# Attention and two mixtures of experts on one core: the first pairs' q sum, the start of their scores, and who does the shared work

## The chip, the cores and the metric

One core of one Trainium2 chip runs the whole program. The metric is device time in microseconds. Three runs of the kernel before took 885.33, 886.92 and 887.47 us; the median is 886.92.

## What is computed

Three layers run one after the other, in float32, on 4 sequences of 576 tokens, 8 heads of 64:

```python
# attention, for every sequence and head
q_d, k_d, v_d = (x.reshape(B, H, Sd, 4, D).mean(axis=3) for x in (q, k, v))
out_d = sm_attn(q_d, k_d, v_d)            # softmax(q_d k_d^T / 8) v_d
out_up = np.repeat(out_d, 4, axis=2)
mask = np.abs(pos[:, None] - pos[None, :]) < 4
out_local = softmax(where(mask, q k^T / 8, -1e9)) v
x = out_up + out_local                    # then to 2304 tokens x 512
# gated layer, 512 -> 1536 -> 512
x = (silu(x @ w_gate) * (x @ w_val)) @ w_out
# one of 8 experts for each token, 512 -> 1024 -> 512
out[mask] = gate_w[mask, None] * (np.maximum(x[mask] @ w1[e], 0) @ w2[e])
```

Down-sampling averages groups of four rows; the scores of the down-sampled attention are products of such averages.

## The kernel before, in words

**Order.** Every piece of work is a generator that yields the engine and the ns it expects to need. A list scheduler in the program (`Sched`, line 92) plays these against each other when the program is built, always taking what can start earliest and, among what is ready, the smallest priority; the instructions are issued in the order so found. At run time each engine goes through its own queue in that order. Line 281 marks work that either VectorE or GpSimd can do ("V"): the planner gives it to the one that would finish first (line 195). Such work is marked `how=True`: the planner does not let it run on VectorE while GpSimd works, nor the other way round (line 187). Copies out of PSUM are fixed to ScalarE.

**Attention.** A pair is two heads of one sequence on 128 partitions; there are 16, four for each sequence. `heads` (line 495) takes five tiles, loads q and k (lines 509, 510), then two layouts of v (lines 513, 514), and creates the tasks of the pair; the planner creates them after it has planned the load of v. The first four pairs (n < 4) use `local_e` and `down_e` in two parts each: part 0 holds the first 256 tokens. `local_e` makes banded scores in units of 58 queries (L724, L730), a softmax (L733 to L747), and turns the result with matmuls (L754). `down_e` sums k in groups of four (L651, L653), makes scores with four strided slices of q accumulated in PSUM (L672), a softmax (L675 to L690), transposes (L697), and a product with v (L707). `down_v` sums v (L547, L549). `piece_e` multiplies the banded weights with v (L782) and adds both (L789). The later pairs use `scores` (where q and k are summed by a reduction, L557), `local`, `down` and `values`.

**Gated layer.** Tokens go in 9 chunks of 256. `x_piece` splits a chunk's x into a high and a low part (L891, L893). The weights come in 6 blocks, each of two pieces of w_gate, w_val and w_out; `decode` (line 377) makes a high and a low part of each piece (L396, L400, L404, L407, L415, L417). `gemm1` (L936 for the very first block, L955) and `gemm2` (L987) use three products for each matmul. For chunks 0 and 1 the blocks alternate between the two chunks, so that one block of weights serves both as it comes in; chunk 2 and later follow. Chunk 2 is the first that needs the second sequence, pairs 4 to 7. `act_h` (L904 to L913) is the nonlinearity between `gemm1` and `gemm2`. Then come routing (line 1059) and the experts.

**Priorities.** `HEAD_P` (line 243) holds one for each pair, `WEIGHT_P` (line 250) one for each weight block: 1.0, 2.0, 3.0, 4.0, 4.5, 4.8. Smaller goes first. Pairs 4 to 7 stand at 1.4, 1.5, 1.6 and 1.7, between block 0 and block 1. Part 1 of a pair stands 0.5 behind part 0. Four pairs can hold tiles at a time.

**Fillers.** `keep_warm` (line 359) lets TensorE multiply zeros wherever the planner finds it free, until the first piece of x exists.

Of the kernel before, what the change touches and what calls it, by code (L numbers as in the profile page):

```python
# [19 lines left out]
ALU = mybir.AluOpType  # L20
# [45 lines left out]
def t_dve(n): return 62 + 1.045 * n  # L66
# [22 lines left out]
BOTH = ("DVE", "POOL")  # L89


class Sched:
# [61 lines left out]
    def advance(self, k, val):  # L154
        self.cur = k
        while True:
            try:
                r = k.gen.send(val)
            except StopIteration:
                break  # L160
            val = None
            if r[0] == "op":
                if k.eng == r[1] == "PE" and k.t == k.end + self.LAT["PE"]:
                    k.t = k.end
                k.ns, k.eng, k.rp, k.how = r[2], r[1], k.prio if r[3] is None else r[3], r[4]
                for eng in BOTH if r[1] == "V" else r[1:2]:
# [29 lines left out]
    def here(self, eng, k):  # L196

        if k.eng != "V":
            return True
        a, b = (self.first(e, k) + n for e, n in zip(BOTH, k.ns))  # L200
        return (a <= b) == (eng == BOTH[0])

    def run(self):
        while True:
            while self.runq:
                self.advance(*self.runq.pop(0))
            best = None
# [12 lines left out]
            start, eng, k = best  # L220
            ns = k.ns
            if k.eng == "V":
                for e, n in zip(BOTH, k.ns):
# [19 lines left out]
HEAD_P = [0.0, 0.1, 0.2, 0.3, 1.4, 1.5, 1.6, 1.7, 16.0, 17.0, 18.0, 19.0, 36.0, 37.0, 38.0, 39.0]  # L243
# [9 lines left out]
def build(tc, a):  # L253
# [241 lines left out]
    def heads(n):  # L495
# [14 lines left out]
        nc.sync.dma_start(out=sk[:, 0:SP6], in_=src[:, SP6:2 * SP6])  # L510
        sc.cur.t -= sc.LAT_DMA
# [3 lines left out]
        pr = sc.cur.prio  # L515
        if n < NV:
            sc.spawn(pr, local_e(n, 0, sq, sk, sv, sa))
            sc.spawn(pr, down_e(n, 0, sq, sk, sd, sa))
            sc.spawn(pr, down_v(n, sk, sd))
            sc.spawn(pr + REST_P, local_e(n, 1, sq, sk, sv, sa))  # L520
            sc.spawn(pr + REST_P, down_e(n, 1, sq, sk, sd, sa))
        else:
            sc.spawn(pr, down_v(n, sk, sd))
            sc.spawn(pr, scores(n, sq, sk, sa))
            sc.spawn(pr, values(n, sq, sk, sv, sa))
# [50 lines left out]
    def down(n, sq, sk, sp):  # L576
# [24 lines left out]
        for h2 in range(2):  # L601
# [7 lines left out]
            yield op("ACT", t_actp(2 * G))  # L609
            nc.scalar.copy(eT[:, h2], tp[:GH, 0:2 * G])  # L610
# [33 lines left out]
    def down_e(n, part, sq, sk, sd, sa):  # L644

        kd, up = (sq[:, SP6 + i * G:SP6 + (i + 1) * G] for i in (1, 2))
# [51 lines left out]
        yield op("ACT", t_actp(4 * w))  # L698
        nc.scalar.copy(eT, tp[:GH, 0:4 * w].rearrange("p (k g) -> p k g", k=2))
# [8 lines left out]
        yield op("ACT", t_actp(w))  # L708
        nc.scalar.copy(up[:, g0:g1], av[:, 0:w])
# [4 lines left out]
    def local_e(n, part, sq, sk, sv, sa):  # L714
# [40 lines left out]
        yield op("ACT", t_actp(k))  # L755
        nc.scalar.copy((sv[:, 640:640 + k], sa[:, 680:680 + k])[part], tp[:, 0:k])
# [7 lines left out]
    def piece_e(n, i, sq, sv, sa):  # L764
# [34 lines left out]
    def values(n, sq, sk, sv, sa):  # L799
# [4 lines left out]
        for jj, t in enumerate(T):  # L804
# [7 lines left out]
            yield op("ACT", t_actp(k))  # L812
            nc.scalar.copy(t, tp[:, 0:k])
# [23 lines left out]
        yield op("ACT", t_actp(G))  # L837
        nc.scalar.copy(up, av)
# [178 lines left out]
    def route_m(c, m, sv, lp):  # L1017
# [5 lines left out]
        yield op("ACT", t_actp(DM), hi)  # L1023
        nc.scalar.copy(row, xp)
# [11 lines left out]
        yield op("ACT", t_actp(DM), hi)  # L1036
        nc.scalar.copy(x2T[:, 0:DM], xp)
# [204 lines left out]
    def load_slot(e, j, tb, xhr, xlr):  # L1242
# [21 lines left out]
        yield op("ACT", t_actp(KD * m), -0.5)  # L1264
        nc.scalar.copy(xhr[:, :, js], pv)
# [166 lines left out]
    def rest_act(e, m, ps, hr):  # L1432
# [8 lines left out]
        for h in range(2):  # L1441
# [5 lines left out]
            yield op("ACT", t_actp(4 * m), -0.5)  # L1447
            nc.scalar.copy(h3[0][:, h], pt[:, 0:4 * m])
# [179 lines left out]
```

## Time and profile before

| | us |
|---|---|
| median of three runs | 886.92 |
| the profiled execution | 885.85 |
| its span, first to last instruction | 884.0 |
| TensorE busy (matmuls) | 865.4 |
| VectorE busy | 482.6 |
| ScalarE busy | 383.5 |
| GpSimd busy | 113.1 |

In the profile PE is TensorE's matmuls, PEld its weight loads, DVE VectorE, ACT ScalarE, POOL GpSimd, SP the queue that issues most loads. Line 672 has 96 matmuls in the code and 192 instructions in the profile: two for each of these float32 products. Matmuls are pipelined and their ends are modelled, so two neighbours can overlap by some ns; the start times are the firmer figures. L672 is line 672 of the kernel above. "<-" names what ended an idle time.

### The profile page before, as it was taken

The page shows a single profiled execution, that of the slowest core. Times are in us where ns is not written, and L with a number is a line of the kernel's source. Part 1 is how long each engine was busy: PE and PEld are TensorE (multiplying, and loading weights), DVE is VectorE, ACT ScalarE, POOL GpSimd, SP SyncE. Part 2 cuts the span into 40 slices and gives each one's busy share as a digit, 9 for nine tenths or more (in the row PEclk, how much of TensorE's full clock was granted, in tenths as well). Part 3 has the DMA queues.
Part 4 walks back from the last instruction along what each step waited for, and adds up shares of the span by engine and source line. Part 5 has one row for each costly group of instructions (what it writes and reads, how often), then busy time and mean ns, then how long its engine had stood idle before and what let it go on. Part 6 is the DMA issues. An engine that isn't in the chain of part 4 may idle for free. (4 is left out here: it accounts for less than half of the span.)

```text
span 884.0 us, 17461 instructions
## 1 busy us (share of the span) xinstructions
PE 865.4 (98%) x7122; PEld 775.7 (88%) x7123; DVE 482.6 (55%) x1163; ACT 383.5 (43%) x923; POOL 113.1 (13%) x115
## 2 busy tenths in 40 slices
PE   9999999999999999999999999999999999999995
PEld 5788889989999999889999999999888888888894
DVE  4999988665476466555333433474455544545210
ACT  2987778543353243333221322355345444444221
POOL 0102200011010010010010000101320330331211
PEclk9999999999999999999999999999999999999998
DMA  8663525312102111120000000354465554553100
GB/s 268 229 206 131 157 90 211 95 39 80 57 26 57 56 27 55 56 80 2 1 25 1 25 1 13 106 190 125 142 207 166 176 175 153 163 183 122 36 27 29
DMA packets 52629, 88.13 MB, mean 100 GB/s; under 512 B 7806, under 2 KB 24574, under 8 KB 52544
## 3 DMA queue, kind: packets, MB, share of 16 engines
q1 hardware_dynamic: 47664, 76.72, 27.1%
q0 software_dynamic: 4160, 9.48, 3.2%
q8 instruction: 57, 0.93, 0.4%
q10 hardware_dynamic: 720, 0.77, 0.3%
q14 instruction: 28, 0.23, 0.1%
HBM read 77.96 MB, written 10.57 MB: 100 GB/s over the span
## 5 line engine op out<-in xcount | busy, mean ns | idle before, releaser
L955 PE MATMUL ps<-xhi,w 128*128 128x256 f32 x1504 | 296.1, 288 | 1.4 <-DVE th L908 0.6
L955 PEld LDWEIGHTS ps<-xhi,w 128*128 128x128 f32 x1504 | 242.2, 191 | 5.2 <-issue 1.3
L955 PE MATMUL ps<-xlo,w 128*128 128x256 f32 x752 | 212.5, 283 | 0.0
L955 PEld LDWEIGHTS ps<-xlo,w 128*128 128x128 f32 x752 | 143.9, 191 | 1.5
L1304 PE MATMUL ps<-xh,w 128*128 128x336 f32 (+1 forms) x512 | 124.0, 315 | 0.0
L987 PE MATMUL x<-w,hh 128*128 128x512 f32 x384 | 120.8, 396 | 0.0
L906 DVE SCALAR_TENSOR_TENSOR th<-th,ps 128x256 f32<-128x256 f32 x108 | 45.0, 418 | 123.9 <-ACT th L904 123.6
L904 ACT ACTIVATE th<-ps 128x256 f32<-128x256 f32 x108 | 41.2, 382 | 150.5 <-PE ps L955 150.0
L1304 PEld LDWEIGHTS ps<-xh,w 128*128 128x128 f32 x512 | 88.2, 188 | 2.2
L1192 DVE TENSOR_TENSOR w<-w,w 128x1024 fp32r<-128x1024 f32 x64 | 76.8, 1217 | 22.7 <-ACT w L1189 22.5
L1304 PE MATMUL ps<-xl,w 128*128 128x336 f32 (+1 forms) x256 | 79.8, 312 | 0.0
L987 PEld LDWEIGHTS x<-w,hh 128*128 128x128 f32 x384 | 68.2, 189 | 11.8 <-issue 0.2
L1314 PE MATMUL x<-w,eh 128*128 128x512 f32 x248 | 78.1, 396 | 0.0
L987 PE MATMUL x<-w,hl 128*128 128x512 f32 x192 | 74.9, 390 | 0.0
L1290 DVE SCALAR_TENSOR_TENSOR el<-ps,eh 128x336 fp32r<-128x336 f32 (+1 forms) x62 | 30.5, 493 | 80.3 <-ACT eh L1288 79.8
L911 ACT CAST hh<-th 128x256 fp32r<-128x256 f32 x108 | 43.6, 404 | 69.3 <-DVE th L908 68.9
L1189 ACT CAST w<-w 128x1024 fp32r<-128x1024 f32 x64 | 65.7, 1046 | 0.0
L1288 ACT ACTIVATE eh<-ps 128x336 fp32r<-128x336 f32 (+1 forms) x62 | 27.4, 442 | 87.8 <-PE ps L1304 86.9
L913 DVE TENSOR_TENSOR hl<-th,hh 128x256 fp32r<-128x256 f32 x107 | 45.6, 427 | 31.9 <-ACT hh L911 31.6
L1314 PEld LDWEIGHTS x<-w,eh 128*128 128x128 f32 x248 | 45.4, 188 | 9.4
L1050 POOL TENSOR_TENSOR sv<-sv,half 128x1 f32<-128x1 f32 x18 | 10.4, 576 | 330.1 <-ACT x L1027 324.2
L1304 PEld LDWEIGHTS ps<-xl,w 128*128 128x128 f32 x256 | 48.2, 188 | 1.3
(250 smaller groups left out, 1349.9 us busy)
## 6 DMA issues: line engine op xcount, KB each, us to landing
w<-w SPq DMA_DIRECT2D x64, 512.0 KB, 3.8
w<-w_gate SPq DMA_DIRECT2D x10, 512.0 KB, 7.1
w<-w_val SPq DMA_DIRECT2D x10, 512.0 KB, 3.6
w<-w_out SPq DMA_DIRECT2D x10, 512.0 KB
w<-qk SPq DMA_DIRECT2D x16, 291.0 KB, 5.3
aw<-qk SPq DMA_DIRECT2D x16, 291.0 KB, 3.5
x2d<-sg SPq DMA_DIRECT2D x18, 256.0 KB, 2.0
w<-vw SPq DMA_DIRECT2D x8, 320.0 KB, 5.8
```

Of the source, the lines that this page charges most:

```text
L904: nc.scalar.activation(th, ps[:, 0:CT], AF.Tanh, scale=0.5)
L906: nc.vector.scalar_tensor_tensor(out=th, in0=th, scalar=1.0, in1=ps[:, 0:CT], op0=ALU.add, op1=ALU.mult)
L911: nc.scalar.copy(hh[:, j].bitcast(F32R), th)
L913: on[e].tensor_tensor(out=hl[:, j].bitcast(F32R), in0=th, in1=hh[:, j].bitcast(F32R), op=ALU.subtract)
L955: nc.tensor.matmul(ps[:, o:o + CT], ww[:, k, fs], xx[:, k, :], start=(k == 0 and n == 0), stop=(k == KD - 1 and n == 2))
L987: nc.tensor.matmul(x2p[c, m], l[:, j, ms], r[:, js], start=(p == 0 and j == 0 and n == 0), stop=(p == NFB - 1 and j == 1 and n == 2))
L1189: nc.scalar.copy(hi.bitcast(F32R), raw)
L1192: nc.vector.tensor_tensor(out=lo.bitcast(F32R), in0=raw, in1=hi.bitcast(F32R), op=ALU.subtract)
L1288: nc.scalar.activation(hh[:, j, 0:n].bitcast(F32R), ps[:, 0:n], AF.Relu)
L1290: nc.vector.scalar_tensor_tensor(out=hl[:, j, 0:n].bitcast(F32R), in0=ps[:, 0:n], scalar=0.0, in1=hh[:, j, 0:n].bitcast(F32R), op0=ALU.max ...
L1304: nc.tensor.matmul(ps[:, 0:n], ww[:, k, fs], xx[:, k, 0:n], start=(k == 0 and t == 0), stop=(k == KD - 1 and t == 2))
L1314: nc.tensor.matmul(yt[:m], l, r, start=(first and n == 0), stop=(last and n == 2))
```

## The change

1. The planner's shared work is a pair of engines instead of one mark. VectorE gets 300 ns added when the two are compared (`BUSY`). Copies out of PSUM to SBUF, fixed to ScalarE before, may now go to VectorE by the same rule (`psum`). This touches lines 610, 699, 709, 756, 813, 838, 1024, 1037, 1265 and 1448 in the same way.
2. Where the next VectorE instruction would have to stand back for GpSimd, the planner takes another that need not.
3. `heads` creates the tasks of a pair as soon as q and k are planned; v has a priority of its own, 0.15 behind, and `piece_e` and the sums of v wait for it.
4. `down_e` sums q in groups of four as it does k, and makes the scores with one matmul instead of four for each tile and half. The half sums of q lie in the unused end of the tile that v is loaded into.
5. Pairs 5, 6 and 7 get the priorities 2.2, 3.2 and 4.2.

```diff
-BOTH = ("DVE", "POOL")
+BUSY = 300.0
...
-        if k.eng != "V":
+        if not isinstance(k.eng, tuple):
             return True
-        a, b = (self.first(e, k) + n for e, n in zip(BOTH, k.ns))
-        return (a <= b) == (eng == BOTH[0])
+        return eng == min(zip(k.eng, k.ns), key=lambda x: self.first(x[0], k) + x[1] + (BUSY if x[0] == "DVE" else 0.0))[0]
...
                 start = self.first(eng, k)
+                if eng == "DVE" and start > max(f, k.t):
+                    loose = [q for q in ks if not q.how and q.t < start]
+                    if loose:
+                        k = min(loose, key=lambda q: (max(q.t, f), q.rp, q.n))
+                        start = self.first(eng, k)
...
-HEAD_P = [0.0, 0.1, 0.2, 0.3, 1.4, 1.5, 1.6, 1.7, 16.0, 17.0, 18.0, 19.0, 36.0, 37.0, 38.0, 39.0]
+HEAD_P = [0.0, 0.1, 0.2, 0.3, 1.4, 2.2, 3.2, 4.2, 16.0, 17.0, 18.0, 19.0, 36.0, 37.0, 38.0, 39.0]
...
     def both(n, prio=None, pool=t_pool):
-        return op("V", (t_dve(n), pool(n)), prio, True)
+        return op(("DVE", "POOL"), (t_dve(n), pool(n)), prio, True)
...
+    def psum(n, prio=None):
+        return op(("ACT", "DVE"), (t_actp(n), t_dve(n)), prio)
+
+    copy = {"ACT": nc.scalar.copy, "DVE": nc.vector.tensor_copy}
...
         nc.sync.dma_start(out=sk[:, 0:SP6], in_=src[:, SP6:2 * SP6])
+        pr, t = sc.cur.prio, sc.cur.t
+        if n < NV:
+            sc.spawn(pr, local_e(n, 0, sq, sk, sv, sa))
+            sc.spawn(pr, down_e(n, 0, sq, sk, sv, sd, sa))
...
         sc.cur.t -= sc.LAT_DMA
-        yield dma(P * NU * D * 4 + GH * 4096)
+        yield op("DMA", t_dma(P * NU * D * 4 + GH * 4096), pr + 0.15)
         nc.sync.dma_start(out=sv[:, 0:NU * D], in_=a["vw"][b, hp])
         nc.sync.dma_start(out=sd[:GH, :], in_=a["vv"][b, hp])
...
+        sc.set(("v", n))
+        sc.spawn(pr, down_v(n, sk, sd))
...
-            k4 = sk[:, 3:3 + S].rearrange("p (g f) -> p g f", f=4)
-            k2 = sa[:, 680:680 + 2 * G].rearrange("p (g f) -> p g f", f=2)
-            e = yield both(2 * G)
-            on[e].tensor_tensor(out=k2, in0=k4[:, :, 0:2], in1=k4[:, :, 2:4], op=ALU.add)
-            e = yield both(G)
-            on[e].tensor_tensor(out=kd, in0=k2[:, :, 0], in1=k2[:, :, 1], op=ALU.add)
+            for x, h, y in ((sk[:, 3:3 + S], sa[:, 680:680 + 2 * G], kd), (sq[:, 0:S], sv[:, 640:640 + 2 * G], qd)):
+                x4, h2 = x.rearrange("p (g f) -> p g f", f=4), h.rearrange("p (g f) -> p g f", f=2)
+                e = yield both(2 * G)
+                on[e].tensor_tensor(out=h2, in0=x4[:, :, 0:2], in1=x4[:, :, 2:4], op=ALU.add)
+                e = yield both(G)
+                on[e].tensor_tensor(out=y, in0=h2[:, :, 0], in1=h2[:, :, 1], op=ALU.add)
...
-        yield op("PE", 980 * k, None, "s")
-        q4 = sq[:, 0:S].rearrange("p (g f) -> p g f", f=4)
+        yield op("PE", 275 * k, None, "s")
         for x, t in enumerate(ts):
-            for i in range(4):
-                for h2 in range(2):
-                    r = slice(h2 * D, (h2 + 1) * D)
-                    nc.tensor.matmul(sp[r, x * G:(x + 1) * G], q4[r, t:t + 64, i], kd[r, :], start=(i == 0), stop=(i == 3))
+            for h2 in range(2):
+                r = slice(h2 * D, (h2 + 1) * D)
+                nc.tensor.matmul(sp[r, x * G:(x + 1) * G], qd[r, t:t + 64], kd[r, :], start=True, stop=True)
...
-        yield op("ACT", t_actp(4 * w))
-        nc.scalar.copy(eT, tp[:GH, 0:4 * w].rearrange("p (k g) -> p k g", k=2))
+        eng = yield psum(4 * w)
+        copy[eng](eT, tp[:GH, 0:4 * w].rearrange("p (k g) -> p k g", k=2))
...
         for c in range((b * S + t0) // CT, (b * S + t1 - 1) // CT + 1):
             yield ("wait", ("x32", c))
+        yield ("wait", ("v", n))
```

## Rows read from the trace of the kernel before

**Rows 1.** Page, parts 1 and 2: busy time; busy tenths in 40 slices, and granted clock.

```profile
PE 865.4 (98%) x7122; PEld 775.7 (88%) x7123; DVE 482.6 (55%) x1163; ACT 383.5 (43%) x923; POOL 113.1 (13%) x115
...
DVE  4999988665476466555333433474455544545210
...
PEclk9999999999999999999999999999999999999998
```

**Rows 2.** Windows: stretch, length; busy us of PE, PEld, DVE, ACT, POOL; PEclk, DMA share, GB/s.

```profile
7.00:65.30 58.30, 57.32 (x928) 45.32 (x926) 50.41 (x136) 40.46 (x124) 3.69 (x6) 1.00 0.76 244
36.00:65.00 29.00, 28.21 (x497) 24.88 (x496) 26.96 (x68) 24.82 (x70) 0.86 (x2) 1.00 0.59 180
65.00:110.00 45.00, 43.99 (x460) 39.60 (x457) 42.29 (x94) 34.40 (x94) 13.18 (x11) 1.00 0.48 149
110.00:150.00 40.00, 38.58 (x384) 34.58 (x383) 34.19 (x79) 31.91 (x72) 1.45 (x1) 1.00 0.44 157
```

**Rows 3.** Timeline of PE: start us, us, what; in brackets the idle time before.

```profile
2.06 10.73 PE L369 MATMUL x<-w 128*128 128x512 bf16 x40 [2.06 <-POOL w L365]
12.63 0.30 PE L724 MATMUL ps<-um,cn 128*128 128x320 bf16 x1
...
36.39 0.39 PE L936 MATMUL ps<-xhi,w 128*128 128x256 f32 x1
...
65.28 1.49 PE L955 MATMUL ps<-aw,w 128*128 128x256 f32 x10 [0.19 <-DVE th L908]
```

**Rows 4.** Windows, with the source filter on line 369 (the filler matmuls).

```profile
12.60:36.40 23.80, 4.86 (x17) 1.31 (x16) 1.00 0.88 289
```

**Rows 5.** Windows, with the source filter on line 672, PE alone.

```profile
10.00:36.40 26.40, 7.22 (x96) 1.00 0.89 295
36.40:65.30 28.90, 6.66 (x96) 1.00 0.60 185
```

**Rows 6.** Timeline of PE, two matmul groups of pair 4.

```profile
60.92 0.81 PE L565 MATMUL ps<-w,w 64*64 64x64 f32 x40
...
63.55 0.71 PE L572 MATMUL ps<-w 64*72 64x144 f32 x8
```

**Rows 7.** Timeline of DVE: landings, the first weight decode, one long instruction.

```profile
7.62 0.46 DVE L651 TENSOR_TENSOR w<-w 128x288 f32<-128x288 f32 x1 [2.41 <-DMA w<-qk]
11.24 0.69 DVE L547 TENSOR_TENSOR w<-w 72x512 f32<-72x512 f32 x1 [3.17 <-DMA w<-vv]
...
29.13 0.42 DVE L396 TENSOR_SCALAR sg<-w 128x512 int32<-128x512 int32 x1
...
93.17 1.22 DVE L407 SCALAR_TENSOR_TENSOR w<-w,sg 128x512 int32<-128x512 int32 x1
```

**Rows 8.** Lines by form, DVE, 7 to 65.3 us: count, busy us, mean ns, idle before.

```profile
L407 DVE SCALAR_TENSOR_TENSOR w<-w,sg 128x512 int32<-128x512 int32 x10 | 6.8, 684 | 1.2 <-ACT sg L404 1.1
L417 DVE TENSOR_TENSOR w<-w,w 128x512 fp32r<-128x512 f32 x10 | 6.8, 680 | 0.6 <-ACT w L415 0.5
...
L747 DVE TENSOR_TENSOR w<-w 128x320 f32<-128x320 f32 x8 | 4.1, 516 | 0.0
...
L651 DVE TENSOR_TENSOR w<-w 128x288 f32<-128x288 f32 x4 | 1.8, 440 | 2.4 <-DMA w<-qk 2.4
...
L653 DVE TENSOR_TENSOR w<-w 128x144 f32<-128x144 f32 x3 | 0.9, 299 | 0.0
```

**Rows 9.** Timeline of ACT: the first exponential of the down scores.

```profile
18.08 0.38 ACT L683 ACTIVATE w<-ps,w 128x144 f32<-128x144 f32 x1
```

**Rows 10.** Lines, POOL, 0 to 170 us.

```profile
L417 POOL TENSOR_TENSOR w<-w,w 128x512 fp32r<-128x512 f32 x5 | 7.6, 1530 | 29.2 <-ACT w L415 29.2
...
L690 POOL TENSOR_TENSOR w<-w,w 128x288 f32<-128x288 f32 x1 | 0.7, 667 | 11.9 <-DVE w L688 11.9
```

**Rows 11.** Timeline of POOL.

```profile
90.28 3.55 POOL L417 TENSOR_TENSOR w<-w,w 128x512 fp32r<-128x512 f32 x2 [7.86 <-ACT w L415]
```

**Rows 12.** Waits of PE, 0 to 200 us: total us, times, longest.

```profile
PE ps L955 <- DVE w L417: 0.3, 1, 0.3
```

More of the change, by code (lines that the diff above doesn't have):

```diff
@@ L165, in advance @@
                 k.ns, k.eng, k.rp, k.how = r[2], r[1], k.prio if r[3] is None else r[3], r[4]
-                for eng in BOTH if r[1] == "V" else r[1:2]:
+                for eng in r[1] if isinstance(r[1], tuple) else r[1:2]:
                     self.pend[eng].append(k)
@@ L221, in run @@
             ns = k.ns
-            if k.eng == "V":
-                for e, n in zip(BOTH, k.ns):
+            if isinstance(k.eng, tuple):
+                for e, n in zip(k.eng, k.ns):
                     self.pend[e].remove(k)
@@ L510, in heads @@
         nc.sync.dma_start(out=sk[:, 0:SP6], in_=src[:, SP6:2 * SP6])
+        pr, t = sc.cur.prio, sc.cur.t
+        if n < NV:
+            sc.spawn(pr, local_e(n, 0, sq, sk, sv, sa))
+            sc.spawn(pr, down_e(n, 0, sq, sk, sv, sd, sa))
+            sc.spawn(pr + REST_P, local_e(n, 1, sq, sk, sv, sa))
+            sc.spawn(pr + REST_P, down_e(n, 1, sq, sk, sv, sd, sa))
+        else:
+            sc.spawn(pr, scores(n, sq, sk, sa))
+            sc.spawn(pr, values(n, sq, sk, sv, sa))
         sc.cur.t -= sc.LAT_DMA
-        yield dma(P * NU * D * 4 + GH * 4096)
+        yield op("DMA", t_dma(P * NU * D * 4 + GH * 4096), pr + 0.15)
         nc.sync.dma_start(out=sv[:, 0:NU * D], in_=a["vw"][b, hp])
         nc.sync.dma_start(out=sd[:GH, :], in_=a["vv"][b, hp])
[L515 to L525, printed above, removed]
+        sc.set(("v", n))
+        sc.spawn(pr, down_v(n, sk, sd))
         yield ("wait", ("done", n))
@@ L608, in down @@
                                         ex[:, 2 * h2 + qh, kh * GH:(kh + 1) * GH], ident[:GH, :GH])
-            yield op("ACT", t_actp(2 * G))
-            nc.scalar.copy(eT[:, h2], tp[:GH, 0:2 * G])
+            eng = yield psum(2 * G)
+            copy[eng](eT[:, h2], tp[:GH, 0:2 * G])
             pput(tp)
@@ L642, in local, with down_e @@
         sc.set(("A", n))
-    def down_e(n, part, sq, sk, sd, sa):
-        kd, up = (sq[:, SP6 + i * G:SP6 + (i + 1) * G] for i in (1, 2))
+    def down_e(n, part, sq, sk, sv, sd, sa):
+        qd, kd, up = (sq[:, SP6 + i * G:SP6 + (i + 1) * G] for i in range(3))
         if part == 0:
-            k4 = sk[:, 3:3 + S].rearrange("p (g f) -> p g f", f=4)
-            k2 = sa[:, 680:680 + 2 * G].rearrange("p (g f) -> p g f", f=2)
-            e = yield both(2 * G)
-            on[e].tensor_tensor(out=k2, in0=k4[:, :, 0:2], in1=k4[:, :, 2:4], op=ALU.add)
-            e = yield both(G)
-            on[e].tensor_tensor(out=kd, in0=k2[:, :, 0], in1=k2[:, :, 1], op=ALU.add)
+            for x, h, y in ((sk[:, 3:3 + S], sa[:, 680:680 + 2 * G], kd), (sq[:, 0:S], sv[:, 640:640 + 2 * G], qd)):
[4 more added lines that the diff above has]
+                on[e].tensor_tensor(out=y, in0=h2[:, :, 0], in1=h2[:, :, 1], op=ALU.add)
             sc.set(("kd", n))
@@ L707, in down_e @@
                 nc.tensor.matmul(av[h2 * D:(h2 + 1) * D, 0:w], vd_of(sk)[:, 2 * h2 + kh, :], e3(h2, kh), start=(kh == 0), stop=(kh == 1))
-        yield op("ACT", t_actp(w))
-        nc.scalar.copy(up[:, g0:g1], av[:, 0:w])
+        eng = yield psum(w)
+        copy[eng](up[:, g0:g1], av[:, 0:w])
         pput(av)
@@ L754, in local_e @@
                 nc.tensor.matmul(tp[r, c(u)], A[r, c(u)], ident[r, r], start=True, stop=True)
-        yield op("ACT", t_actp(k))
-        nc.scalar.copy((sv[:, 640:640 + k], sa[:, 680:680 + k])[part], tp[:, 0:k])
+        eng = yield psum(k)
+        copy[eng]((sv[:, 640:640 + k], sa[:, 680:680 + k])[part], tp[:, 0:k])
         pput(tp)
@@ L811, in values @@
                 nc.tensor.transpose(tp[:, i * P:(i + 1) * P], sa[:, j * P:(j + 1) * P], ident)
-            yield op("ACT", t_actp(k))
-            nc.scalar.copy(t, tp[:, 0:k])
+            eng = yield psum(k)
+            copy[eng](t, tp[:, 0:k])
             pput(tp)
@@ L836, in values @@
                 nc.tensor.matmul(xp[r, q:q + UQ - o], sv[r, u * D:(u + 1) * D], T[u // 4][r, i + o:i + UQ], start=True, stop=True)
-        yield op("ACT", t_actp(G))
-        nc.scalar.copy(up, av)
+        eng = yield psum(G)
+        copy[eng](up, av)
         t0 = 0
@@ L1022, in route_m @@
         xp = x2p.pop((c, m))
-        yield op("ACT", t_actp(DM), hi)
-        nc.scalar.copy(row, xp)
+        eng = yield psum(DM, hi)
+        copy[eng](row, xp)
         sc.spawn(sc.cur.prio, store_x2(c, m, row))
@@ L1035, in route_m @@
         x2T = last_T[m] if last_T else (yield ("get", tcls))
-        yield op("ACT", t_actp(DM), hi)
-        nc.scalar.copy(x2T[:, 0:DM], xp)
+        eng = yield psum(DM, hi)
+        copy[eng](x2T[:, 0:DM], xp)
         sc.put(x2cls(c), xp)
@@ L1263, in load_slot @@
         js = slice(j * P, j * P + m)
-        yield op("ACT", t_actp(KD * m), -0.5)
-        nc.scalar.copy(xhr[:, :, js], pv)
+        eng = yield psum(KD * m, -0.5)
+        copy[eng](xhr[:, :, js], pv)
         yield op("DVE", t_dve(KD * m), -0.5)
@@ L1446, in rest_act @@
                 nc.tensor.transpose(pt[:, (f % 4) * m:(f % 4 + 1) * m], hr[:m, f * P:(f + 1) * P], ident[:m, :m])
-            yield op("ACT", t_actp(4 * m), -0.5)
-            nc.scalar.copy(h3[0][:, h], pt[:, 0:4 * m])
+            eng = yield psum(4 * m, -0.5)
+            copy[eng](h3[0][:, h], pt[:, 0:4 * m])
             yield op("DVE", t_dve(4 * m), -0.5)
```

## The prediction

> **What bounds the kernel now.** I read the page first. TensorE is busy 98% of the span at a granted clock of 1.00 (the 2.4 GHz level) in all slices but the last; VectorE's slices are at 8 or 9 tenths early on and near 5 later [rows 1]. So the kernel is TensorE work laid end to end, and a change can win in two ways: less TensorE work, or less TensorE time that is filler or idle.
>
> The table by stage says where either can be had. From 36 us on TensorE hardly idles: 0.8 us of 29, 1.0 of 45, 1.4 of 40 up to 150 us. From 7 to 65.3 us VectorE works 50.4 of 58.3 us and ScalarE 40.5, while GpSimd does 3.7 [rows 2]. Early on two engines are full at the same time and a third is nearly empty.
>
> The order of TensorE's work [rows 3] shows the stages. The first pair's scores start at 12.63 us, after forty filler matmuls; the first weight product (L936) starts at 36.39; the dense stream of L955 begins at 65.28. Between 12.6 and 36.4 us there are 17 more filler matmuls, 4.86 us [rows 4]; one belongs to the opening block, so I count 16, 4.5 us. Fillers stop when the planner sees the first x, so this is TensorE time that waits for others.
>
> I treat 65.28 us as the marker. Behind it the same weight products follow nearly without gaps, so what the marker moves by, the end moves by.
>
> **Part 1, q summed ahead.** Today a pair's down-sampled scores multiply four strided slices of q by the summed k (L672); the new code sums q first and multiplies once. Line 672 has 192 matmul instructions: 7.22 us before 36.4, 6.66 us after [rows 5]. A quarter stays, 48. At the same mean that is 13.88 x 3/4 = 10.4 us of TensorE removed. The neighbours bound the new instructions: L565, 40 small ones in 0.81 us (20 ns each), and L572, 8 of the same 64x144 shape in 0.71 us (89 ns, entering and leaving the tiled mode included) [rows 6]. So 48 cost 1.0 to 4.3 us and 9.6 to 12.9 us go; I take 10.4, nearest the row of the same shape.
>
> What it adds: two sums for each of four pairs, like those of k at L651 and L653, 440 and 299 ns on VectorE [rows 8], so 4 x 0.74 = 3.0 us if all stay there. No row shows them on the path; the same-shaped k sums are the measure. For the first pair they stand in front of its down scores, but the local scores don't need them and run first.
>
> **Part 2, scores without v.** The tasks were created after the v load was planned, and the planner prices that load at 622,592 bytes / 310 = 2.0 us. In the trace k has landed at 7.62 us (L651 starts), v at 11.24 (L547 ends its wait) [rows 7], while TensorE turns filler until 12.63. I take 2.0 us earlier for the first scores; the bounds are 0, should something else hold them, and 3.6, the gap between the two landings. On SP's queue the next pair's q and k now pass v of the pair before: that v lands up to 594,000 / 310 = 1.9 us later. Behind it are only the v sums and, through them, the exponential at L683, which first runs at 18.08 us [rows 9]; 11.24 + 1.9 leaves it about 4 us for two short sums, so this costs nothing. If that cover were gone, those 1.9 us would stand in front of L683.
>
> **Part 3, shared work leans to GpSimd, copies out of PSUM to whichever of ScalarE and VectorE is freer.** A 300 ns penalty on VectorE sends a 320-element shared step to GpSimd whenever GpSimd is free (685 against 396 + 300 ns by the planner's formulas), a 288-element one when VectorE is 0.1 us late, and a 512-element one when it is 0.37 us late. In 7 to 65.3 us the candidates on VectorE are L747 (8, 4.1 us), L417 (10, 6.8 us), L651 and L653 (2.7 us), the new q sums, and smaller ones of lines 547, 549, 690 and 893 [rows 8]. On GpSimd the same step costs about twice or less: L417 1530 against 680 ns, L690 667 ns for 288 elements [rows 10]. Some 47 us of GpSimd are free there, so at most about 24 us of VectorE could move, and at least none. Nothing in the trace says how much; I take 9 us (some 17 us of GpSimd), about a third of the candidates, since the penalty only tips steps for which GpSimd is free at that moment. The copies are counted at nothing: ScalarE is not the fuller engine here, and VectorE, which would take them, is.
>
> **Part 4, pairs 4 to 7 one per weight block.** They are needed only by the third chunk. From 65 to 150 us TensorE idles 2.4 us in all [rows 2], which caps the gain; I count nothing, and keep 2.4 for the low end. Their loads hold tiles that the weights also need, so an unlucky order can cost as much.
>
> **The sum.** Three limits on the marker:
> - TensorE: 65.3 - 2.0 - 10.4 - 4.5 (filler) - 0.8 (idle) = 47.6 us.
> - VectorE: it did 50.4 us between 7.0 and 65.3 and idled 7.9, nearly all ahead of the first pair. New: 50.4 + 3.0 - 9 = 44.4 us of work and 7.9 - 2.0 = 5.9 idle, so 7.0 + 44.4 + 5.9 = 57.3 us.
> - ScalarE: 40.5 us of work; begun with the first scores at 10.6 it would end at 51.1 without idle time. Weight decoding, which waits for VectorE too, starts only at 29.13 us [rows 7], behind the pairs; with the pairs earlier it can start earlier.
>
> The latest is VectorE's: 57.3, which is 8.0 us ahead of 65.3. So VectorE takes over as the bound of the head, and of TensorE's 10.4 + 2.0 us some 4 turn into filler or waits. From the marker on TensorE is dense again and carries the 8.0 us to the end. The profiled execution took 885.85 us (span 884.0 and 1.85 around it), 1.07 under the median: 885.85 - 8.0 = 877.9, as a median **878.9 us**.
>
> A price in the later stages: L913, 256 elements, will at times go to GpSimd too, some 0.3 us longer each (L690 there: 667 ns for 288 elements [rows 10], L651 of the same length on VectorE 440 [rows 8]). Its product is used one block later, behind several us of matmuls, so I count nothing; without that cover it would be 0.3 us at each of the 7 later chunk ends, 2 us.
>
> **Rivals.**
> - *TensorE's limit is reached* (chance 0.17). If GpSimd takes 19 us or more of VectorE's work, the marker falls towards 47.6: 17.7 us of gain, 869.2; with part of it 869 to 875. For it: 47 empty us of GpSimd. Against: chains inside a pair get longer with every step on the slower engine.
> - *GpSimd and VectorE get in each other's way* (0.12). L407 takes 684 ns on average [rows 8], but the one at 93.17 us took 1.22 us [rows 7], while two L417 were on GpSimd from 90.28 to 93.83 [rows 11]. If every moved step holds up one VectorE step by 0.5 us, 17 or 18 steps hand back 9 us: 888, within the band of no change. The Trainium skill says it in "SBUF — State Buffer", section "Who interferes with whom": a VectorE instruction with two SBUF inputs and a GpSimd one that reads SBUF exclude each other, and the later one waits for the whole of the other. On that rule the trace agrees in direction, 1.22 us against 684 ns. Against a full loss: the planner already keeps most such pairs apart, and the average shows it; reductions and PSUM readers, a large part of the head's VectorE work, can be put beside GpSimd's.
> - *Only half of it moves* (0.07): 4.5 us instead of 9, marker 61.8, 883.4.
> - *The scores still wait for v* (0.08). The first half sums of q are written into the tile that v lands in. If that write waits for the load, the early start is lost: 2.0 us, 880.9. No row here shows such a write.
> - *Slower: weights arrive late through GpSimd* (0.06). The last step of each weight piece, L417, is shared; on GpSimd it is 0.85 us longer. It decides where the pieces are just in time: 5 later blocks x 3 matrices x 0.85 = 12.8 us, net +4.8, 891.7. For it: TensorE's waits before 200 us include L417. Against: that wait is 0.3 us, once [rows 12].
>
> **How the numbers follow.** The forecast (875.5 to 882) has 0.50, the rivals 0.17, 0.12, 0.07, 0.08 and 0.06. A measurement of this kernel can tell about 0.3% from no change, 2.7 us. Faster by more than that: 0.50 + 0.17 + 0.08 + 0.05 of the half move + 0.03 of the interference case = 0.83; within it 0.10; slower 0.07. For the range I leave out 0.1 at each end: the low end reaches into TensorE's limit, 872; the high end through the half move into the interference case, 886.
>
> **What the new profile should show.** L672 with 48 instructions and 3 to 4 us; the first L724 near 10.6 us; the first dense L955 near 57; GpSimd's total well above 113 us, with L747 and L417 among its rows; VectorE's total down by several us; TensorE's busy total down by about 8. Wrong would be: dense L955 starting at 63 or later; TensorE waiting for GpSimd's L417 or L893; long cases of L407, L396 or L631 in number; a granted clock under 1.00 in the head because TensorE has run out of work; or the 8 us present at the marker and gone at 180 us.

## The result, and the profile after

The changed kernel takes 879.53 us (median of five runs, 877.43 to 881.37), the kernel before 887.21 beside it: a ratio of 0.9905, interval 0.9886 to 0.9925, 7.7 us less in medians. The forecast was 878.9.

The page, parts 1 and 2, after:

```profile
PE 858.2 (98%) x6976; PEld 768.3 (88%) x6977; DVE 476.2 (54%) x1132; ACT 381.2 (43%) x914; POOL 153.0 (17%) x163
...
DVE  4799998566564365663342423666455544545210
...
POOL 4443300022112010020010000201320330331111
PEclk9899999999999999999999999999999999999998
```

TensorE's busy time fell by 7.2 us and the span by 6.5. VectorE lost 6 us and GpSimd gained 40. The clock row has an 8 early on, where the kernel before has none.

By stage, to be read against [rows 2]; the column behind GpSimd's is the granted clock:

```profile
7.00:61.50 54.50, 51.13 (x783) 38.34 (x782) 42.37 (x111) 36.56 (x122) 28.01 (x38) 0.91 0.84 260
7.00:65.30 58.30, 54.94 (x848) 41.94 (x847) 46.17 (x121) 39.88 (x129) 29.94 (x40) 0.91 0.85 261
30.00:40.00 10.00, 9.19 (x173) 7.55 (x169) 8.28 (x23) 8.74 (x30) 3.33 (x5) 0.89 0.23 92
40.00:50.00 10.00, 8.03 (x138) 6.85 (x138) 7.90 (x21) 7.96 (x24) 2.58 (x4) 0.77 0.80 238
50.00:60.00 10.00, 9.72 (x135) 8.26 (x130) 9.74 (x20) 6.64 (x21) 4.91 (x4) 0.83 1.00 347
110.00:150.00 40.00, 40.00 (x360) 36.55 (x359) 36.89 (x84) 34.57 (x76) 0.21 (x1) 1.00 0.50 166
150.00:200.00 50.00, 50.00 (x437) 46.47 (x436) 30.06 (x86) 23.63 (x64) 5.06 (x6) 1.00 0.19 59
200.00:420.00 220.00, 220.00 (x2100) 203.00 (x2099) 121.61 (x343) 78.92 (x251) 26.30 (x30) 1.00 0.15 48
```

VectorE's work between 7 and 65.3 us went from 50.4 to 46.2 us, GpSimd's from 3.7 to 29.9. But TensorE idled more in that stretch than before (3.4 us against 1.0), and from 30 to 60 us its mean clock was 0.77 to 0.89. From 110 to 420 us it idles no longer. The kernel before did, 1.4 us up to 150 and 1.7 in these two stretches:

```profile
150.00:200.00 50.00, 49.29 (x393) 45.93 (x393) 32.53 (x90) 26.32 (x66) 3.29 (x4) 1.00 0.22 67
200.00:420.00 220.00, 219.03 (x2130) 201.58 (x2129) 124.95 (x359) 80.78 (x258) 16.22 (x20) 1.00 0.16 50
```

TensorE's order, to be read against [rows 3]:

```profile
2.06 9.28 PE L378 MATMUL x<-w 128*128 128x512 bf16 x31 [2.06 <-POOL w L374]
11.18 0.30 PE L731 MATMUL ps<-um,cn 128*128 128x320 bf16 x1
...
38.04 1.29 PE L790 MATMUL ps<-w,w 64*64 64x58 f32 x20
...
45.31 0.39 PE L944 MATMUL ps<-xhi,w 128*128 128x256 f32 x1
...
47.45 0.77 PE L790 MATMUL ps<-w,w 64*64 64x58 f32 x20
...
61.50 0.87 PE L963 MATMUL ps<-aw,w 128*128 128x256 f32 x6
```

The first scores start 1.45 us earlier (11.18 against 12.63). The first weight product, L944 here, starts 8.9 us *later* (45.31 against 36.39). The dense stream starts 3.8 us earlier (61.50 against 65.28). The rows at 38.04 and 47.45 us show the clock: twenty matmuls of the same form take 1.29 us in one place, where the granted clock is 0.50, and 0.77 in the other, where it is 1.00.

The starts of equal work, counted in the two traces (the stream is L955 before, L963 after; its 337th instruction comes when the pairs of the second sequence are done):

| | before | after | difference |
|---|---|---|---|
| first of the stream | 65.3 | 61.5 | -3.8 |
| 97th | 86.5 | 86.6 | 0.1 |
| 241st | 122.6 | 119.5 | -3.1 |
| 337th | 146.5 | 141.9 | -4.6 |
| first expert product | 605.1 | 598.6 | -6.5 |
| span | 884.0 | 877.5 | -6.5 |

So in these two executions 4.6 us come from the head, 1.9 between 147 and 605 us, and nothing in the experts. Ahead of the first, the 241st and the 337th the two kernels have issued the same matmuls, but for the 144 instructions of L672 that are gone and two fillers. Ahead of the 97th the changed kernel has issued 52 more of the pairs' own, so there the two cannot be compared.

### The profile page after: what moved, and what is told of

Read it like the earlier page. It is cut to its first block, busy times and chain, and to the rows that moved or that the text cites. A ratio compares the mean times of both kernels' runs of the same rounds, so it can differ in the third digit from the quotient of the medians.

```text
span 877.5 us, 17216 instructions
## 1 busy us (share of the span) xinstructions
PE 858.2 (98%) x6976; PEld 768.3 (88%) x6977; DVE 476.2 (54%) x1132; ACT 381.2 (43%) x914; POOL 153.0 (17%) x163
## 5 line engine op out<-in xcount | busy, mean ns | idle before, releaser
L963 PE MATMUL ps<-xhi,w 128*128 128x256 f32 x1504 | 295.9, 288 | 1.7 <-POOL w L426 1.3
L963 PEld LDWEIGHTS ps<-xhi,w 128*128 128x128 f32 x1504 | 242.2, 191 | 5.4 <-POOL w L426 1.5
L963 PE MATMUL ps<-xlo,w 128*128 128x256 f32 x752 | 212.5, 283 | 0.0
L963 PEld LDWEIGHTS ps<-xlo,w 128*128 128x128 f32 x752 | 144.0, 191 | 1.4
L1058 POOL TENSOR_TENSOR sv<-sv,half 128x1 f32<-128x1 f32 x18 | 10.4, 577 | 290.5 <-ACT x L1035 285.0
L921 DVE TENSOR_TENSOR hl<-th,hh 128x256 fp32r<-128x256 f32 x94 | 39.7, 424 | 30.9 <-ACT hh L919 30.8
L1337 POOL DMA_INDIRECT out<-sg,tb x23 | 23.3, 1012 | 172.3 <-ACT sg L1329 160.7
```

The costliest lines, as they stand in the source:

```text
L921: on[e].tensor_tensor(out=hl[:, j].bitcast(F32R), in0=th, in1=hh[:, j].bitcast(F32R), op=ALU.subtract)
L963: nc.tensor.matmul(ps[:, o:o + CT], ww[:, k, fs], xx[:, k, :], start=(k == 0 and n == 0), stop=(k == KD - 1 and n == 2))
```

## The experiments

All twelve were timed in five rounds beside the kernel before, on one chip for each set. The first four share a chip, so do the fifth to the eighth and the ninth to the eleventh; the times of different sets differ, so the ratios are what to compare. Ratios are to the kernel before, intervals in brackets; a difference of 0.001 is 0.9 us, and differences in us between kernels are worked out from the ratios. Each window and timeline shows one execution. The first four, the seventh to the ninth, the eleventh and the twelfth edit the changed kernel (0.9905), the others the kernel before.

**Fillers go on** until the first piece of chunk 1.

```diff
-        while ("x", 0, 0) not in sc.ev:
+        while ("x", 1, 0) not in sc.ev:
```

> The changed kernel, with the fillers going on until the first piece of chunk 1 exists instead of the first piece of chunk 0. In the changed kernel the granted clock is 0.50 from 37.7 to 44.5 us and from 51.4 to 54.8 us, just after the last filler at 32.7 us; L790's groups of 20 take 1.2 us there against 0.7. Theory A (the lower clock lengthens the path): the clock stays at 1.00 from 30 to 60 us, the dense stream of the second block starts 2 to 5 us earlier and the kernel takes 875 to 877.5. Theory B (the stretch waits for the weight decode on VectorE and ScalarE anyway): the clock stays at 1.00 and the time stays at 878.5 to 880.5.

Measured: 0.9894 (0.9873 to 0.9915). Windows of this kernel:

```profile
40.00:50.00 10.00, 8.13 (x179) 6.42 (x179) 9.95 (x27) 8.71 (x27) 2.70 (x4) 0.96 0.90 291
50.00:60.00 10.00, 10.00 (x111) 8.99 (x115) 9.10 (x18) 6.59 (x20) 4.70 (x5) 0.87 1.02 340
60.00:80.00 20.00, 16.80 (x173) 14.13 (x164) 19.97 (x42) 16.36 (x42) 3.27 (x4) 0.91 0.41 133
```

and TensorE's longest wait for another engine's work on the stream:

```profile
PE ps L963 <- ACT w L424: 2.4, 2, 2.1
```

The clock fell all the same, to 0.96, 0.87 and 0.91: the planner sets fillers where it believes TensorE free, and the waits that occur lie elsewhere. So this run does not tell what the lower clock costs; its time, 879.69 us, is the changed kernel's.

**No lean** to GpSimd; the copies keep theirs.

```diff
-... + (BUSY if x[0] == "DVE" else 0.0))[0]
+... + (BUSY if x[0] == "DVE" and k.eng[0] == "ACT" else 0.0))[0]
```

> The changed kernel without the 300 ns on VectorE for work that GpSimd can share; the copies out of PSUM keep theirs. Theory A (the prediction's: VectorE is the limit of the head and the lean moves it): GpSimd does 4 to 10 us instead of 30 between 7 and 65 us, VectorE 49 to 53, and the kernel takes 885 to 888. Theory B (GpSimd is so full before 32 us that the steps of the weight decode that may not run beside it are held back): the first weight decode starts before 30 us instead of at 33.4, the first weight product before 40 instead of at 45.3, and the kernel takes 875 to 880.

Measured: 0.9914 (0.9893 to 0.9934). Window, first decode on VectorE, and first products:

```profile
7.00:65.30 58.30, 54.23 (x831) 41.26 (x830) 52.60 (x142) 40.47 (x130) 13.29 (x20) 1.00 0.78 249
```

```profile
28.69 0.39 DVE L405 TENSOR_SCALAR sg<-w 128x512 int32<-128x512 int32 x1
```

```profile
37.18 0.39 PE L944 MATMUL ps<-xhi,w 128*128 128x256 f32 x1
...
58.15 1.22 PE L963 MATMUL ps<-aw,w 128*128 128x256 f32 x9
```

VectorE did 52.6 us in that stretch, 6.4 more than in the changed kernel, and the dense stream still began 3.4 us earlier (58.15). Theory A is out: VectorE's sum of work does not set the head. Theory B holds for the decode (28.69, products from 37.18); the time, 880.83 us, lies just past its 880.

**The old q**: four strided slices, no q sums, the rest of the change kept.

```diff
-            for x, h, y in ((sk[:, 3:3 + S], sa[:, 680:680 + 2 * G], kd), (sq[:, 0:S], sv[:, 640:640 + 2 * G], qd)):
+            for x, h, y in ((sk[:, 3:3 + S], sa[:, 680:680 + 2 * G], kd),):
...
-                nc.tensor.matmul(sp[r, x * G:(x + 1) * G], qd[r, t:t + 64], kd[r, :], start=True, stop=True)
+            for i in range(4):
...
+                    nc.tensor.matmul(sp[r, x * G:(x + 1) * G], q4[r, t:t + 64, i], kd[r, :], start=(i == 0), stop=(i == 3))
```

> The changed kernel with the down scores made by four strided slices of q again, without the q sums. Theory A (TensorE's work in the head counts in full): 144 more matmul instructions of 67 ns, 9.6 us, less what stands in for fillers ahead of 45 us (18 fillers, about 4.5 us): 884 to 889. Theory B (the head is bound by VectorE, ScalarE and GpSimd, and TensorE's work there hides): 880 to 882, with fewer fillers and no lower clock, because TensorE has more to do.

Measured: 884.43 us, 0.9959 (0.9943 to 0.9974), 4.8 us more than with the new q. Theory A's range holds.

**Tasks wait for v** again, the loads keep the new order.

```diff
+        yield op("DMA", t_dma(P * NU * D * 4 + GH * 4096), pr + 0.15)
...
         if n < NV:
             sc.spawn(pr, local_e(n, 0, sq, sk, sv, sa))
...
-        yield op("DMA", t_dma(P * NU * D * 4 + GH * 4096), pr + 0.15)
```

> The changed kernel with the tasks of a pair created after its load of v has been planned, as before; the loads keep their new order. Theory A (an earlier start of the scores is an earlier end): the first scores start near 15 us instead of 11.2, since the next pair's q and k now go ahead of v, and the kernel takes 3 to 4 us longer, 882 to 884. Theory B (the path starts with the weight loads and their decode, at 33 us): 878.5 to 880.5.

Measured: 886.31 us, 0.9969 (0.9954 to 0.9984), 5.7 us more. First scores and first product on TensorE, first decode on VectorE:

```profile
14.55 0.30 PE L731 MATMUL ps<-um,cn 128*128 128x320 bf16 x1
...
47.51 0.39 PE L944 MATMUL ps<-xhi,w 128*128 128x256 f32 x1
```

```profile
37.12 0.42 DVE L405 TENSOR_SCALAR sg<-w 128x512 int32<-128x512 int32 x1
```

The scores start 3.4 us later, the decode 3.7, the first product 2.2. Theory A, and more than it asked for. But these scores also start 1.9 us later than in the kernel before (12.63): with the loads in their new order, a pair that waits for v waits longer than it used to. So part of the 5.7 us can be the price of that order, and the changed kernel with the old order of the loads as well was not run.

**The kernel before with the q sums alone.**

```diff
-            e = yield both(2 * G)
-            on[e].tensor_tensor(out=k2, in0=k4[:, :, 0:2], in1=k4[:, :, 2:4], op=ALU.add)
...
+            for x, h, y in ((sk[:, 3:3 + S], sa[:, 680:680 + 2 * G], kd), (sq[:, 0:S], sv[:, 640:640 + 2 * G], qd)):
...
-                    nc.tensor.matmul(sp[r, x * G:(x + 1) * G], q4[r, t:t + 64, i], kd[r, :], start=(i == 0), stop=(i == 3))
...
+                nc.tensor.matmul(sp[r, x * G:(x + 1) * G], qd[r, t:t + 64], kd[r, :], start=True, stop=True)
```

> The kernel before with the q sums alone: one matmul instead of four for each tile and half, everything else as before. Theory A (TensorE is the limit after 36 us and its work there goes out in full): the half of L672 behind 36.4 us goes, 6.66 x 3/4 = 5.0 us, and the part ahead turns into fillers: 880.5 to 884, the ratio 0.993 to 0.997. Theory B (VectorE, 97% busy there and with 3.0 us more to do, sets the pace): no change or slower, 886 to 890.

Measured: 891.25 us, 1.0021 (1.0004 to 1.0039). Theory B, and past its 890. The start of the stream, a window and the wait:

```profile
60.17 4.79 PE L953 MATMUL ps<-aw,w 128*128 128x256 f32 x39
```

```profile
60.00:80.00 20.00, 14.31 (x168) 12.04 (x168) 19.87 (x45) 12.75 (x43) 3.50 (x2) 0.84 0.38 121
```

```profile
PE ps L809 <- DVE w L641: 5.3, 1, 5.3
```

The stream starts 5.1 us earlier than in the kernel before, and the kernel gains nothing. In this execution, the longest of its twelve, TensorE waits 5.7 of these 20 us, 5.3 of them for the last softmax step of a later pair on VectorE, which is busy 19.9 of the 20; and the clock averaged 0.84.

**The kernel before with the early start alone.**

```diff
-        sc.cur.t -= sc.LAT_DMA
-        yield dma(P * NU * D * 4 + GH * 4096)
...
+        sc.cur.t -= sc.LAT_DMA
+        yield op("DMA", t_dma(P * NU * D * 4 + GH * 4096), pr + 0.15)
...
+        sc.set(("v", n))
+        sc.spawn(pr, down_v(n, sk, sd))
...
+        yield ("wait", ("v", n))
```

> The kernel before with the early start alone: tasks created without waiting for v, loads in the new order, no lean, no q sums, the old priorities. Theory A (the early start is worth by itself what it lost when taken out of the changed kernel, 5.7 us): 881 to 884, the ratio 0.992 to 0.996. Theory B (it is worth something only together with less TensorE work, because TensorE is already full from 15 us on): 885 to 888.

Measured: 889.44 us, 1.0018 (1.0003 to 1.0032). Theory B, and slightly past it. TensorE's longest wait for another engine, 2.1 us, is for a weight piece from ScalarE (L419).

**The old priorities** of pairs 5 to 7.

```diff
-HEAD_P = [0.0, 0.1, 0.2, 0.3, 1.4, 2.2, 3.2, 4.2, ...
+HEAD_P = [0.0, 0.1, 0.2, 0.3, 1.4, 1.5, 1.6, 1.7, ...
```

> The changed kernel with the old priorities of pairs 5 to 7 (1.5, 1.6, 1.7). The prediction counts the new ones at nothing, within 2.4 us: 877 to 882. Theory B (they keep the weight decode ahead of pairs that nothing waits for): the wait for weights between 65 and 110 us grows from 1.9 us to 4 or more and the kernel takes 882 to 886.

Measured: 880.80 us, 0.9922 (0.9893 to 0.9951), within the prediction's allowance. TensorE's longest wait for another engine is now for a pair's softmax on GpSimd:

```profile
PE ps L616 <- POOL w L608: 3.2, 1, 3.2
```

**The lean only behind 60 us** of TensorE's planned time.

```diff
-... + (BUSY if x[0] == "DVE" else 0.0))[0]
+... + (BUSY if x[0] == "DVE" and (k.eng[0] == "ACT" or self.free["PE"] > 60000.0) else 0.0))[0]
```

> The changed kernel with the 300 ns for shared work counted only once TensorE's planned time has passed 60 us. Without the lean anywhere the first weight decode began at 28.7 us instead of 33.4 and the second weight block's first product came 5.6 us sooner (81.0 against 86.6), but by the 336th product of the stream that lead was gone (143.1 against 141.9). Theory A (the lean costs in the head and pays behind it): the lead is kept, 873 to 877. Theory B (what the head gains is lost again to a different order of the pairs whatever the lean): 878 to 882.

Measured: 877.76 us, 0.9878 (0.9852 to 0.9904), between the two theories. First products:

```profile
37.13 0.39 PE L944 MATMUL ps<-xhi,w 128*128 128x256 f32 x1
...
58.85 1.34 PE L963 MATMUL ps<-aw,w 128*128 128x256 f32 x9 [0.61 <-DVE enT L473]
```

The 337th of the stream starts at 140.6 us, the first expert product at 597.2, each 1.3 to 1.4 us ahead of the changed kernel. This is the lowest ratio measured, though its interval meets the changed kernel's.

**Copies on ScalarE alone.**

```diff
-        return op(("ACT", "DVE"), (t_actp(n), t_dve(n)), prio)
+        return op(("ACT",), (t_actp(n),), prio)
```

> The changed kernel with the copies out of PSUM on ScalarE alone, as before. The prediction counts this part at nothing: 878 to 881. Theory B (it is what removes the waits of 1.7 us between 150 and 420 us, since all kernels with the free choice lost less than 0.95 us there and the kernels without it lost up to 2.7): the stretch from the 336th product of the stream to the end grows from 735.6 to 737 us or more, and the kernel takes 881 to 884.

Measured: 879.95 us, 0.9901 (0.9881 to 0.9921). The copies are worth nothing that can be told from zero, as predicted. The stretch from the 337th to the end is 736.2 us (735.6 in the changed kernel, 737.5 before), under the 737 that theory B asked for. Yet TensorE idles 1.0 us between 200 and 420 us again, as in the kernel before:

```profile
200.00:420.00 220.00, 218.97 (x2085) 201.21 (x2084) 120.11 (x342) 80.04 (x252) 26.29 (x30) 1.00 0.16 48
```

**The kernel before with q sums and early start together**, that is with the two edits just shown, and still without lean, second choice, new priorities or copies on VectorE.

> The kernel before with the q sums and the early start together, and nothing else of the change. Alone each of them left the kernel at 1.002 of its time; taken out of the changed kernel each cost 5 to 6 us. Theory A (they need each other: the early start feeds the work, the q sums make room on TensorE for it): 880 to 884, the ratio 0.991 to 0.996. Theory B (both need the relief of VectorE by the lean, the free copies or the other choice next to GpSimd): 886 to 891.

Measured: 885.92 us, 0.9974 (0.9954 to 0.9993), between the two theories. Windows and the longest wait for another engine, from an execution 4.8 us above that median:

```profile
40.00:50.00 10.00, 7.82 (x117) 5.92 (x117) 10.00 (x28) 9.88 (x37) 1.47 (x3) 0.84 0.19 56
50.00:60.00 10.00, 10.00 (x143) 8.55 (x141) 5.67 (x15) 5.97 (x15) 1.80 (x2) 0.64 0.58 172
```

```profile
PE ps L814 <- DVE w L645: 3.1, 1, 3.1
```

The two together win some 2.3 us where each alone is 1.6 to 1.9 us longer, so they do need each other; the other 6 us of the change need something more.

**The planner's tie**: a VectorE step that must stay clear of GpSimd may start 1 ns before GpSimd is free, and so is chosen ahead of GpSimd's next step, not behind it.

```diff
         if eng == "DVE" and k.how and self.free["POOL"] > t:
-            t = self.free["POOL"] + 1
+            t = self.free["POOL"] - 1
```

> The changed kernel with one number changed in the planner: a VectorE step that must not run beside GpSimd becomes startable 1 ns before GpSimd is free instead of 1 ns after, so that it is no longer passed over for as long as GpSimd has another step ready. Theory A (under the lean the weight decode is held back by an unbroken row of GpSimd steps): the first decode starts before 31 us instead of 33.4, the first weight product before 41 instead of 45.3, the clock does not fall before 60 us, and the kernel takes 875 to 878. Theory B (the decode is late because its priority is below the pairs', not because it is passed over): the first decode stays at 33 us or later, and the time at 878.5 to 881.

Measured: 877.74 us, 0.9893 (0.9868 to 0.9917). First decode, first products:

```profile
30.24 1.25 DVE L405 TENSOR_SCALAR sg<-w 128x512 int32<-128x512 int32 x2
```

```profile
38.18 0.39 PE L944 MATMUL ps<-xhi,w 128*128 128x256 f32 x1
...
59.56 5.20 PE L963 MATMUL ps<-aw,w 128*128 128x256 f32 x42
```

Theory A holds for the decode: with the lean in place, one number moved the first decode from 33.42 to 30.24 and the first weight product from 45.31 to 38.18. The time lies in theory A's range, but the interval does not part it from the changed kernel, so the 7.1 us by which the first product came sooner were worth nothing that can be told from zero. The clock did still fall: its mean is 0.86 from 40 to 50 us and 0.97 from 50 to 60.

**Without the second choice** on VectorE.

```diff
-                if eng == "DVE" and start > max(f, k.t):
-                    loose = [q for q in ks if not q.how and q.t < start]
...
```

> The changed kernel without the planner's second choice on VectorE, so that a VectorE step that has to stand back for GpSimd is waited for instead of passed over. The q sums and the early start alone gave 0.9974; with everything 0.9905; the lean, the copies and the priorities could each be taken out for less than 1.5 us. Theory A (the second choice is what makes the difference, because without it VectorE stands idle beside GpSimd): VectorE idles more between 8 and 33 us, and the kernel takes 884 to 887. Theory B (lean, copies, priorities and second choice all relieve the same engine, and any of them will do): 879 to 882.

Measured: 879.00 us, 0.9891 (0.9863 to 0.9920). Theory B: not needed either. The first decode:

```profile
29.98 0.73 DVE L400 TENSOR_SCALAR sg<-w 128x512 int32<-128x512 int32 x2
```

It comes 3.4 us sooner than in the changed kernel, so with the second choice the decode comes later too. In this execution the granted clock is 1.00 all through the head, and its 337th of the stream starts at 141.8 us, against 141.9 in the changed kernel, whose clock fell twice.

**Together.** Taken out of the change one by one, the early start costs 5.7 us (with the new order of the loads kept) and the q sums 4.8, with intervals (0.9954 to 0.9984, 0.9943 to 0.9974) that lie clear of the change's (0.9886 to 0.9925). Lean, copies, priorities and second choice cost 0.8, -0.4, 1.5 and -1.2, none of it clear. Yet q sums and early start without any of these four reach 0.9974 only. So one or more of the four is needed, and each can be spared while the other three stand. Which pairs of them would do was not tried and stays open. One more reading was not tested: every edit also makes the planner find another order of all the work. The seven kernels here that differ from the changed one in one setting of the planner or the fillers lie between 0.9878 and 0.9922, up to 0.0027 from its 0.9905. So losses as small as those of the two edits alone (0.0021, 0.0018) can be another order of the work and nothing else.

## Why the prediction was right, and where it was not

The number, the sign and the range hold: 7.7 us in the medians, predicted 8.0. That the number fits so well is in part luck, since the way to it does not hold. The sum put 8.0 us at the marker and let them pass to the end; 3.8 came at the marker and 6.5 at the end of the span, and the lean, on which the whole 8.0 rested, proved worth nothing that can be told from zero. What the gain does need, by the experiments, is the q sums and the early start together, and one or more of the other four parts.

**Part 1, the q sums.** L679, the old L672, against [rows 5]:

```profile
10.00:36.40 26.40, 3.73 (x40) 1.00 0.87 251
36.40:65.30 28.90, 0.66 (x8) 0.82 0.81 256
```

It is 4.4 us for 48 instructions where 192 took 13.88: 9.5 us gone, predicted 10.4, and just outside the bounds of 9.6 to 12.9. An instruction now takes 91 ns, the price of the L572 row of the same shape (89 ns), which I named as nearest and then did not take. Their worth, 4.8 us in the third experiment, is about half of the work that went; the prediction let some 4 us of the two steps' 12.4 turn into filler or waits.

**Part 2, the early start, was mis-sized.** The first scores moved by 1.45 us, predicted 2.0. But in the fourth experiment the tasks' wait for v cost 5.7 us, part of which can belong to the new order of the loads. I priced the first pair alone: the q and k of later pairs pass a load of v as well, and no pair's tasks wait for its own v any more. That this makes up the rest is argued, not shown. The cover I named for the later v held: the first exponential of the down scores starts at 18.31 us, 18.08 before.

**The sum's VectorE limit is the step that failed.** "The latest is VectorE's: 57.3" took VectorE's busy time for a limit. The dense stream began at 61.50. Of the sum's terms up to there the work was near (42.4 us against 44.4), the idle time was not: 12.1 us against 5.9. The second experiment goes further. The lean did about what I counted, 6.4 us off VectorE and 16.6 onto GpSimd between 7 and 65.3 us, where I had 9 and 17. By the sum a kernel without it has 53.4 us of VectorE work, a marker at 66.3 and no gain at all; it had an earlier stream, 58.15, and kept 0.9914.

**The marker is the other step that failed.** "What the marker moves by, the end moves by" is refuted both ways: the kernel without the lean starts its stream 3.4 us ahead of the changed kernel and is not faster, and the kernel before with the q sums alone starts it at 60.17, 5.1 us ahead of the kernel before, and gains nothing. Between the marker and the 337th of the stream the pairs of the second sequence still have to be done, and what they wait for is not in the sum.

Two readings of the prediction were also off, without deciding it: GpSimd has 54.6 us free in that stretch (58.3 less 3.7), not 47; and of VectorE's 7.9 idle us 5.3 lie ahead of 13.7 us, not nearly all.

What came late in the changed kernel was the first weight decode,

```profile
33.42 0.75 DVE L405 TENSOR_SCALAR sg<-w 128x512 int32<-128x512 int32 x2
```

at 33.42 us against 29.13 in [rows 7]. GpSimd's steps from 7 to 65.3 us, and the window from 8 to 33:

```profile
L754 POOL TENSOR_TENSOR w<-w 128x320 f32<-128x320 f32 x8 | 7.1, 888 | 4.7 <-DVE w L695 3.2 <-DVE w L752 1.5
L697 POOL TENSOR_TENSOR w<-w,w 128x144 f32<-128x144 f32 (+1 forms) x8 | 5.3, 668 | 8.8 <-DVE w L695 8.8
...
L660 POOL TENSOR_TENSOR w<-w 128x288 f32<-128x288 f32 x4 | 2.7, 664 | 2.2 <-DMA w<-qk 2.2
```

```profile
8.00:33.00 25.00, 24.70 (x404) 16.19 (x402) 16.86 (x50) 13.56 (x54) 18.90 (x28) 1.00 0.99 294
```

GpSimd worked 18.9 of the 25 us from 8 to 33. The first step of a decode may not run on VectorE beside it, by the planner's rule. With the lean, GpSimd has one such step after another; the tie let GpSimd go first, and the second choice gave VectorE other work meanwhile. Taking away any one of the three brought the decode forward: 28.69 without the lean, 30.24 with the tie turned round, 29.98 without the second choice. None of the three changed the time by an amount clear of noise, so the late decode is not shown to cost anything, and the lean that I counted as 9 us of relief is worth 0.8 us by the second experiment, which is not told from zero.

**What I counted at nothing made up for some of it.** From the 337th of the stream to the first expert product the changed kernel is 1.9 us faster; TensorE's 1.0 us idle from 200 to 420 us and 0.7 from 150 to 200 have gone. The kernels with one part taken out have between 0.4 us (copies on ScalarE) and all of it (old q, old priorities), one execution each, and the kernel with more fillers has 0.6. So no run here shows its cause; another order of the later pairs' steps is the nearest reading, and only argued. That part of the gain I had not foreseen.

**The rivals.** *In each other's way*: L754 took 888 ns on GpSimd on average and 0.72 us in its usual case; L697 has a case of 1.11 us where 0.66 is usual. The longest L754 began while VectorE was in a sum of two tiles:

```profile
26.41 0.68 DVE L556 TENSOR_TENSOR w<-w 72x512 f32<-72x512 f32 x1
```

```profile
26.48 1.55 POOL L754 TENSOR_TENSOR w<-w 128x320 f32<-128x320 f32 x1
```

The Trainium skill says in "SBUF — State Buffer", section "Who interferes with whom", that a VectorE instruction with two SBUF inputs contends with a GpSimd instruction that reads SBUF; this row agrees in direction. What such meetings cost the kernel no run here shows. *Weights late through GpSimd*: seen once, and small, the second of these two waits of TensorE (the first is for a pair's softmax):

```profile
PE ps L761 <- POOL w L754: 1.5, 1, 1.5
PE ps L963 <- POOL w L426: 1.3, 1, 1.3
```

1.3 us for L426, the old L417, against the 12.8 that the rival needed. *TensorE's limit*: not reached. *The scores still wait for v*: no; they start at 11.18, and GpSimd's first v sum waits for v until 13.78:

```profile
13.78 1.27 POOL L556 TENSOR_TENSOR w<-w 72x512 f32<-72x512 f32 x1 [1.33 <-DMA w<-vv]
```

**The signs I named.** L679 with 48 instructions, GpSimd above 113 us (153.0) and VectorE down several us came. The stream near 57 and 8 us at the marker did not. And two signs of "wrong" did: a clock under 1.00 in the head, and TensorE waiting for GpSimd's L426, the old L417, if only for 1.3 us.

## What to carry to other kernels

Where two engines are full at once, an edit that is good in the whole can be worth nothing alone: here each of two gained nothing (1.0021, 1.0018), both together 0.9974, and with the rest of the change 0.9905. An engine's busy time in a stretch is a lower bound on its end, not a forecast: taking 6.4 us off VectorE was worth nothing that can be told from zero. Nor is an earlier step a gain until the end has moved: the first weight product came 7.1 us sooner by one number in the planner, without a clear gain. A marker serves only if the work behind it waits for nothing else; the first product of the stream was none. And in a list scheduler look at ties: a rule of "after the other is free" can pass a step over as long as the other has one more ready.

## What the hardware showed that I had not expected

In the head of the changed kernel TensorE's granted clock went from 2.4 to 1.2 GHz twice, from 37.7 to 44.5 and from 51.4 to 54.8 us, 10.2 us in all:

```profile
30.00:37.70 7.70, 7.00 (x131) 5.36 (x127) 6.17 (x19) 6.50 (x22) 3.33 (x5) 1.00 0.30 119
37.70:44.50 6.80, 6.70 (x111) 6.20 (x113) 4.99 (x15) 5.69 (x19) 0.30 (x1) 0.50 0.35 111
51.40:54.80 3.40, 3.40 (x52) 2.69 (x52) 3.40 (x7) 2.73 (x6) 1.13 (x2) 0.51 1.00 348
```

The last filler starts at 32.9 us. Ahead of the first fall TensorE did short tiled products with waits of up to 0.45 us between them; ahead of the second it waited 1.5 us for L754. At the lower level twenty products of L790 took 1.29 us against 0.77. The fillers of the first experiment moved the fall and did not prevent it. Whether the fall costs this kernel time is not shown: in the profiled executions of the second, eighth, ninth and twelfth kernels the clock stays at 1.00 in the head, and their medians are 877.8 to 880.8 us, the changed kernel's 879.5.

The clock also differs between executions of one program. The seventh kernel's six spans are 882.5 us at a mean clock of 0.991, 880.9 at 0.992, 877.9 and 879.2 at 0.993, and 876.8 and 878.4 at 0.995; the eleventh's are 877.3 and 879.9 at 0.991, 875.9 at 0.992, 875.0 and 875.2 at 0.995 and 874.3 at 0.996. In these two, more time at the low level goes with a longer span; whether it makes it longer, or both come from the same waits, no run here separates. In the third kernel executions at 0.995 spread from 881.3 to 886.1, so the clock is not the whole of the spread.
